# Gamma multiplied into B instead of C, a shorter chain of parameters and a new order in a fused S5 and H3 kernel

## The chip, the cores and the metric

The kernel runs on one core of a Trainium2 chip. Its engines are TensorE (PE, matmuls into the accumulators PSUM), VectorE (DVE), ScalarE (ACT), GpSimd (POOL) and SyncE (SP, which here only issues DMAs); ACT can issue DMAs as well. The metric is the device time of one execution in microseconds (us), the median of three runs.

## The reference

Two layers are computed on 2048 rows of 640 columns, and their results are put side by side (bf16, 2048 x 1280).

```python
Lam_bar = exp(dt * Lam)                              # A: a diagonal state-space layer (S5), 640 complex states
B_bar = ((Lam_bar - 1.0) / Lam)[:, None] * Bmat
Bu = einsum("bld,pd->blp", x, B_bar)
h[t] = Lam_bar * h[t - 1] + Bu[t]                    # 2048 steps
y_A = 2.0 * einsum("blp,dp->bld", h, Cmat).real + x * Dskip

kv = shift_conv(k, shift_k) * v                      # B: H3, four taps, then a long convolution of length 2048
y = irfft(rfft(kv, 4096) * rfft(ssm_k, 4096))[:2048] + kv * ssm_D
y_B = q * y
out = concatenate([y_A, y_B], axis=-1)
```

The factor of a state, 2(Lam_bar - 1)/Lam with the 2 of the output taken in, is called gamma below. Since the recurrence is diagonal, gamma can be multiplied into B or into C.

## The kernel before, in words

All data lie in one SBUF tile, `arena`, cut into named parts (A, BT, RR, Y, T, ...), and all accumulators in one PSUM tile, `acc`, of eight banks. `build` makes a list of some 800 operations; each names the engines that may run it and the pieces of `arena` that it reads and writes. `Program.depend` (L92) finds from the pieces which operation has to follow which. The string `ORDER` gives the order: every entry is the number of an operation, the engine (T for TensorE, V for VectorE, A for ScalarE, G for GpSimd, S for SyncE) and the first PSUM bank. `Program.emit` (L122) writes the program of each engine in this order, with a wait wherever a predecessor is on another engine. Every engine and every DMA queue runs what it has strictly in that order. Line numbers in the profile are of the operation's code; helpers that copy or scale (L198, L199) stand for many operations.

Part A, in the order of its data:

- The parameters (`params`, L338 on): TensorE turns Lambda and log_dt into columns (L356), VectorE copies them (L358), and a chain of small operations on 128 x 10 numbers makes the phases, the powers `al` of Lam_bar, gamma (`cf`), and from these the matrices that TensorE uses: `RR` (L436) for powers of Lam_bar, `GM` for gamma.
- `load_B` (L482): each of five blocks of B is loaded and turned by TensorE with an identity (L496, two groups of five transposes a block), evicted by L498 into `BT`. `warm` (L511) is eight matmuls ahead of it.
- The up-sweep: `up2` (L552, the base matmuls x·B, evicted by L568), `up1` (ten base matmuls and two of L571, evicted by L590) and `up0` (L552, L571, L612) build sums over 16 rows. The coarse scan (`coarse`, L619) swaps halves on TensorE (L639, L640), multiplies by cosines and sines on VectorE (L642 to L653) and scans (L647). The down-sweep (`down`, L672, L673; added by L690 or L692) fills in all states.
- `scale_C` (L531): ten groups of eight matmuls (L543) multiply gamma, as `GM`, into the loaded C; L547 evicts them into `CT`.
- `project` (L696): for each of 16 row sets ten matmuls for each half with C (L711), VectorE adds x·D (L715, with L701), and a DMA stores the rows (L719). Row set 13 comes last and is cut in two halves.

Part B makes kv (taps L198, sums L794 and L795), writes it to DRAM and reads it back in another layout, and does the long convolution by two matmul stages (`s1` L830 or L835, `s2` L854, evicted by L840 and L867), a product (L878 to L885) and two stages back (`r2` L899, `r1` L920, evicted by L904 and L932); L944 stores it. The same stages transform ssm_k. A group of `s1` has a wide form (16 matmuls over 128 rows, L830) and a narrow one (32 over 64 rows, L835); a lower-case t in `ORDER` asks for the narrow one. GpSimd makes the tables of phases (L289, L291, L327, L330) and takes some of the products.

The operations around `up2` are mixed with part B's kv on VectorE and ScalarE; `s1` and `s2` of ssm_k run between the up-sweep's and down-sweep's groups; part B's remaining stages run between the 16 projections.

## Time and profile before

| what | value |
|---|---|
| median of three runs | 193.33 us (193.14 to 193.49) |
| span of the profiled execution | 195.7 us |
| VectorE, ScalarE, GpSimd, share of the span | 84%, 72%, 40% |
| DMA, mean rate | 30.15 MB, 154 GB/s |
| base matmuls of the up-sweep (L552) | 220 in 47.8 us |
| projection (L711) | 320 in 45.7 us |
| gamma into C: TensorE (L543), VectorE's share of evictions (L547) | 80 in 4.3 us, 5 in 3.9 us |

The page of the profile gives busy time by engine and groups of instructions by line: the engine, the operation, its output and input, shapes (partitions x elements), count, busy time, mean ns of one, and the idle time of the engine in front of them with what released it. Timelines have the start, the duration, and the same names. In the windows a stretch of time has its length, and busy time and instructions of each engine.

### The profile page before, as it was taken

What the parts mean: (1) busy time and instruction counts of PE and PEld (TensorE: products, weight loads), DVE (VectorE), ACT (ScalarE), POOL (GpSimd) and SP (SyncE); (2) the same over time, 40 slices, a digit from 0 to 9 for tenths busy, and PEclk for the clock granted to TensorE, in tenths of its full rate; (3) what the DMA queues carried; (4) which work ended last, traced back from release to release, by engine and by line L of the source; (5) the groups of instructions that cost most, each with busy time, mean ns of one, the idle gap of its engine ahead of it and who ended that gap; (6) DMA issues with size and microseconds to landing.
All of it is one profiled execution on the core that took longest, in us unless ns stands there. A gap on an engine that the chain in (4) does not pass through costs nothing.

```text
span 195.7 us, 7455 instructions
## 1 busy us (share of the span) xinstructions
PE 181.7 (93%) x3297; PEld 120.1 (61%) x3300; DVE 165.3 (84%) x228; ACT 140.9 (72%) x170; POOL 78.1 (40%) x62
## 2 busy tenths in 40 slices
PE   7699699999999999889998999999999999999980
PEld 2586334444455666565676675557678776977750
DVE  4686999337999898999999999999999999969840
ACT  2499936999999899999988999888747750750000
POOL 8979940530030000196805480876050209302020
PEclk9999979999999999999999999999999999999998
DMA  5999869989699999979993899511199970536985
GB/s 153 259 195 176 135 131 151 185 131 135 129 249 183 243 244 123 156 149 152 126 138 147 208 189 158 106 36 35 35 219 184 189 155 3 134 107 157 211 192 154
DMA packets 103786, 30.15 MB, mean 154 GB/s; under 512 B 97482, under 2 KB 103114, under 8 KB 103754
## 3 DMA queue, kind: packets, MB, share of 16 engines
q1 hardware_dynamic: 103004, 28.86, 81.1%
q10 hardware_dynamic: 750, 0.82, 1.4%
q8 instruction: 26, 0.43, 0.9%
q14 instruction: 6, 0.05, 0.1%
HBM read 12.30 MB, written 7.86 MB: 103 GB/s over the span
## 4 chain that ended last, share of the span: by engine, by line
PE 69%; ACT 10%; DMA 8%; DVE 5%; issue 4%; SPq 2%; ACTq 0%; DVEq 0%
PE acc L711 21%; PE acc L552 19%; PE acc L899 6%; PE acc L854 5%; DMA arena<-in_B_ssm_k_dram 4%; PE acc L571 4%; ACT arena L867 4%; PE acc L835 4%; PE acc L673 3%; PE acc L920 3%; DMA arena<-in_A_B_re_dram 2%; SPq L761 2%; PE acc L830 2%; ACT arena L498 2%; PE acc L672 1%
## 5 line engine op out<-in xcount | busy, mean ns | idle before, releaser
L552 PE MATMUL acc<-arena 128*128 128x512 bf16 (+1 forms) x220 | 47.8, 375 | 1.9 <-DVE arena L402 1.9
L711 PE MATMUL acc<-arena 128*128 128x320 bf16 x320 | 45.7, 299 | 0.0
L867 ACT CAST arena<-acc 128x960 bf16<-128x960 f32 (+1 forms) x40 | 35.2, 907 | 7.0 <-PE acc L854 6.4
L711 PEld LDWEIGHTS <-arena 128*128 128x128 bf16 x320 | 30.4, 98 | 12.6 <-ACT arena L867 0.4
L552 PEld LDWEIGHTS <-arena 128*128 128x128 bf16 x220 | 21.9, 102 | 23.7 <-DVE arena L402 2.2
L840 ACT CAST arena<-acc 128x1024 bf16<-128x1024 f32 x32 | 31.1, 1027 | 2.0 <-PE acc L835 1.5
L904 ACT CAST arena<-acc 128x1024 bf16<-128x1024 f32 x16 | 15.6, 1029 | 10.8 <-PE acc L899 10.8
L854 PE MATMUL acc<-arena 128*64 128x160 bf16 x512 | 22.2, 235 | 0.4 <-ACT arena L867 0.3
L701 POOL TENSOR_TENSOR arena<-arena 128x640 bf16<-128x640 bf16 x8 | 11.7, 1473 | 26.1 <-DMA arena<-in_A_x_dram 26.1
L854 PEld LDWEIGHTS <-arena 128*64 128x64 bf16 x512 | 17.9, 109 | 5.8 <-issue 1.7
L794 POOL TENSOR_TENSOR arena<-arena 128x2048 bf16<-128x2048 bf16 x2 | 8.5, 4246 | 28.3 <-DVE arena L198 28.3
L715 DVE TENSOR_TENSOR arena<-acc,arena 128x640 bf16<-128x640 f32 (+1 forms) x17 | 13.1, 782 | 6.3 <-PE acc L711 6.1
L883 POOL TENSOR_TENSOR arena<-arena 128x1280 bf16<-128x1280 bf16 x4 | 11.3, 2824 | 16.7 <-DVE arena L881 11.0
L794 DVE TENSOR_TENSOR arena<-arena 128x2048 bf16<-128x2048 bf16 x13 | 16.0, 1233 | 1.3 <-ACT arena L199 1.2
L840 DVE CAST arena<-acc 128x1024 bf16<-128x1024 f32 x8 | 9.7, 1221 | 6.8 <-PE acc L835 6.7
L673 PE MATMUL acc<-arena 128*128 128x512 bf16 (+2 forms) x50 | 12.8, 327 | 0.0
L835 PEld LDWEIGHTS <-arena 64*64 64x64 bf16 x960 | 9.3, 107 | 4.9 <-issue 1.3
L881 POOL TENSOR_TENSOR arena<-arena 128x1280 bf16<-128x1280 bf16 x3 | 7.8, 2617 | 11.0 <-ACT arena L867 6.1
L932 DVE TENSOR_TENSOR arena<-acc,arena 128x960 bf16<-128x960 f32 (+1 forms) x12 | 11.9, 1036 | 0.0
L878 DVE TENSOR_TENSOR arena<-arena 128x2560 bf16<-128x2560 bf16 x8 | 11.9, 1483 | 0.0
L835 PE MATMUL acc<-arena 64*64 64x64 bf16 x960 | 11.3, 194 | 0.4 <-ACT arena L840 0.2
L692 DVE TENSOR_TENSOR arena<-acc,arena 128x1024 bf16<-128x1024 f32 (+1 forms) x10 | 11.1, 1137 | 0.5 <-PE acc L673 0.5
(143 smaller groups left out, 309.9 us busy)
## 6 DMA issues: line engine op xcount, KB each, us to landing
out_dram<-arena SPq DMA_DIRECT2D x31, 160.0 KB, 3.2
arena<-in_B_ssm_k_dram SPq DMA_DIRECT2D x8, 320.0 KB, 4.8
kv_rows<-arena SPq DMA_DIRECT2D x5, 512.0 KB, 3.9
arena<-kv_rows SPq DMA_DIRECT2D x16, 160.0 KB, 4.4
arena<-in_A_x_dram SPq DMA_DIRECT2D x16, 160.0 KB, 3.4
arena<-in_B_q_dram SPq DMA_DIRECT2D x8, 320.0 KB, 5.5
arena<-in_A_B_re_dram ACTq DMA_DIRECT2D x3, 160.0 KB, 3.4
arena<-in_A_B_im_dram SPq DMA_DIRECT2D x3, 160.0 KB, 3.5
```

The source lines that it names most:

```text
L552: e.matmul(o, lhsT=self.BT[j][:, d, :], rhs=self.XP[:, d, lo:lo + n], start=(d == 0), stop=(d == 4), skip_group_check=True)
L673: e.matmul(B[:, o], lhsT=c.RR[:, n, j, :], rhs=fr(j, q, k), start=not by_pe, stop=True, skip_group_check=True)
L711: e.matmul(B[:, 512 * (b - b0):512 * (b - b0) + 320], lhsT=lh[j], rhs=self.CT[:, j, 320 * b:320 * b + 320], start=(j == 0), stop=(j == 9))
L715: P.add(f"ev_C{i}", {PDVE: dve(320 * (b1 - b0))}, lambda e, B, part=part, n=b1 - b0: e.tensor_tensor(out=part.rearrange("p (b n) -> p b n" ...
L794: P.add(f"ca{d}_{j}", tt, lambda e: e.tensor_tensor(out=t1, in0=t1, in1=t2, op=ALU.add), outs=[t1], ins=[t1, t2])
L835: e.matmul(B[64 * b:64 * b + 64, 512 * l + 64 * i:512 * l + 64 * i + 64], lhsT=lh[i][ps], rhs=F[ps, b, 64 * l:64 * l + 64], start=True, st ...
L840: P.add(f"e1{what}{hf}_{u}", {PACT: act(1024), PDVE: dve(1024)}, lambda e, B: c.CP[e](out=out, in_=(B.rearrange("p (l n s k) -> p k s l n" ...
L854: e.matmul(B[64 * s:64 * s + 64, 512 * b + 160 * i:512 * b + 160 * i + 160], lhsT=c.W[:, k, 64 * b:64 * b + 64], rhs=self.AS[hf][:, k, 160 ...
L867: c.CP[e](out=out, in_=b.rearrange("p r (k j n) -> p r k j n", k=n, j=4) if nj > 1 else b.rearrange("p r (k x) -> p r k x", k=n))
L878: P.add(f"pp{hf}", n1, lambda e: e.tensor_tensor(out=pt, in0=X, in1=Yk, op=ALU.mult), outs=[pt], ins=[X, Yk])
L904: P.add(f"er2{hf}_{u}", {PACT: act(1024), PDVE: dve(1024)}, lambda e, B: c.CP[e](out=out, in_=B.rearrange("p (s n b) -> p b s n", s=2, n=4 ...
L932: e.tensor_tensor(out=Q, in0=B.rearrange("p (g x) -> p g x", g=2)[:, :, 0:80 * n].rearrange("p g (x n) -> p g x n", n=40), in1=Q, op=ALU.mult)
```

## The change

Gamma moves from C to B. A block of B is no longer turned with an identity; each half of its rows is multiplied by a 64 x 128 matrix made of gamma, so that turning and scaling are one step. It is 20 matmuls over 64 rows a block (two groups, of 16 and 4) with results in f32, where there were ten transposes. The evictions are of 1024 and 256 elements where there were two of 640. `scale_C` with its 80 matmuls and ten evictions goes. In its place `place_C` copies C into the states' layout: eight copies over 64 rows, five on VectorE (four of 2560 elements, one of 640) and three on ScalarE (640 each).

The chain of parameters gives 15 columns where it gave 10 (five more for the layout of B's rows), joins steps by two-scalar operations and `scalar_tensor_tensor`, makes powers by squaring (`rq`) instead of five exponentials, and makes the sine that gamma needs on ScalarE ahead of the phases' tables. `gm` is five small spreads, one a block, instead of one big one. The sign of the phase offsets turns, so the coarse scan adds where it subtracted, and the other way round.

Stores of the output (`st_A`, `st_B`) may be issued by ScalarE. In the new order 11 of 33 are. `ORDER` is new throughout; GpSimd loses three operations (two taps' sums and the spread of the scan's factor r16), VectorE gets them. Of 40 groups of `s1`, 17 are wide where 10 were; five of these seven come after the first projection. The last group of the up-sweep's L552 and two of five groups of `s2` that stood ahead of the coarse scan's first swap stand behind it now on TensorE.

```diff
-    ("PV", 60), ("SMALL", 1400)):
+    ("PV", 90), ("SMALL", 1500)):
...
+    sg = f(10).rearrange("p (x k) -> p x k", x=2)
+    for x, sc in ((0, PI), (1, TWO_PI)):
+        P.add("sg", {A: .2}, lambda e, x=x, sc=sc: e.activation(out=sg[:, x], in_=fr[:, 10:15], func=FN.Sin, scale=float(sc * EPS1)),
+              outs=[sg[:, x]], ins=[fr[:, 10:15]])
...
+    def gm(k):
+        P.add(f"gm{k}", {V: .42}, lambda e: e.tensor_tensor(
+            out=c.GM[:, k], in0=bc(c.E.rearrange("p (o m) -> p o m", o=1), [128, 4, 64]),
+            in1=bc(c4[:, :, k:k + 1], [128, 4, 64]), op=ALU.mult), outs=[c.GM[:, k]], ins=[c.E, c4[:, :, k:k + 1]])
+    for k in range(5):
+        gm(k)
...
-        for r in range(2):
-            g, part = P.group(1), raw[:, 640 * r:640 * r + 640]
...
-                for d in range(5):
-                    e.transpose(out=B.bitcast(bf16)[:, 128 * d:128 * d + 128], in_=part[:, 128 * d:128 * d + 128], identity=idn)
+        for d0, n in ((0, 4), (4, 1)):
+            g = P.group(2)
...
+                for d in range(d0, d0 + n):
+                    for r in range(2):
+                        for j in range(2):
+                            ps = slice(64 * j, 64 * j + 64)
+                            o = 512 * j + 128 * (d - d0)
+                            e.matmul(B[:, o:o + 128], lhsT=raw[ps, 640 * r + 128 * d:640 * r + 128 * d + 128],
+                                     rhs=c.GM[ps, k, 2 * r:2 * r + 2, :].rearrange("p x m -> p (x m)"), start=(r == 0), stop=(r == 1),
+                                     skip_group_check=True, tile_position=(64 * j, 0))
...
-    def scale_C(self, a, h):
...
+    def place_C(self):
+
+        c, P = self.c, self.c.P
+        T4 = self.CT.rearrange("p (a e) d -> p a e d", e=2)
+        for part, a0, n in ((0, 0, 4), (1, 4, 1)):
+            for e_ in range(2):
+                for r in range(2):
+                    to, fro = slice(64 * r, 64 * r + 64), slice(64 * e_, 64 * e_ + 64)
+                    out, src = T4[to, a0:a0 + n, e_], self.CRa[part][fro, r]
+                    P.add(f"mvC{part}{e_}{r}", {PDVE: .16 + .00026 * 640 * n, PACT: act(640 * n)}, lambda e, out=out, src=src: c.CP[e](out=out, in_=src),
+                          outs=[out], ins=[src])
...
-            P.add(f"st_A{i}", {PSP: .5}, lambda e, dst=dst, part=part: e.dma_start(out=dst, in_=part), ins=[part], nbytes=128 * 640 * (b1 - b0))
+            P.add(f"st_A{i}", {PSP: .5, PACT: .5}, lambda e, dst=dst, part=part: e.dma_start(out=dst, in_=part), ins=[part], nbytes=128 * 640 * (b1 - b0))
...
-    "162A0 98G0 48G0 73V0 0V0 11G0 75S0 5G0 4T0 12V0 13V0 76A0 6G0 14V0 163S0 17V0 36G0 168A0 74S0 31V0 1T1 32V0 24G0 15V0 55V0 "
+    "24G0 48G0 11G0 5G0 6G0 19V0 152S0 139V0 73V0 75S0 39G0 12V0 13V0 17V0 32V0 30V0 147S0 31V0 7V0 74A0 55V0 20G0 33V0 76A0 51V0 "
```

The first place is VectorE during the up-sweep's first pass. Before, its evictions are L568; L232, L256, L412 and L274 are small operations on tables and parameters, L498 evicts B.

```order
L232 TENSOR_TENSOR arena<-arena 128x64
L256 TENSOR_TENSOR arena<-arena 128x4
L412 TENSOR_SCALAR arena<-arena 128x10
L568 CAST arena<-acc 128x2x2x256
L402 MEMSET arena 64x1
L274 TENSOR_TENSOR arena<-arena 128x256
L498 COPY arena<-acc 128x10x64
L568 CAST arena<-acc 128x2x2x256
```

In the new kernel the same evictions are L588; L814 is a sum of taps of kv, L449 makes `al`, L456 spreads it into `RR`, and L272, L306, L256 and L274 are tables.

```order
L272 TENSOR_SCALAR arena<-arena 128x64
L306 TENSOR_SCALAR arena<-arena 128x192
L814 TENSOR_TENSOR arena<-arena 128x2048
L256 TENSOR_TENSOR arena<-arena 128x4
L274 TENSOR_TENSOR arena<-arena 128x256
L449 TENSOR_TENSOR arena<-arena 128x80
L588 CAST arena<-acc 128x2x2x256 x2
L456 TENSOR_TENSOR arena<-arena 128x1280
L588 CAST arena<-acc 128x2x2x256 x2
```

The evictions of this pass stand in one block behind the tables and `al`; before, small operations and evictions took turns, and B's own evictions stood among them.

The second place is VectorE between the coarse scan and the first projection's sum (L715 before, L735 after). Before: L547 evicts gamma·C, L642 and L653 belong to the scan, L692 to the down-sweep, L840 and L867 to ssm_k's transform, L198 to the taps.

```order
L547 CAST arena<-acc 128x2x320
L642 TENSOR_TENSOR arena<-acc,arena 128x640
L653 TENSOR_TENSOR arena<-arena 128x5x128
L692 TENSOR_TENSOR arena<-acc,arena 128x4x256
L547 CAST arena<-acc 128x2x320 x2
L840 CAST arena<-acc 128x64x2x8
L198 TENSOR_SCALAR arena<-arena 128x2048 x2
L701 TENSOR_TENSOR arena<-arena 128x640
L692 TENSOR_TENSOR arena<-acc,arena 128x256
L547 CAST arena<-acc 128x2x320 x2
L867 CAST arena<-acc 128x2x3x160 x2
L198 TENSOR_SCALAR arena<-arena 128x2048
```

After: L567 copies C, L673 is the scan's last step, L712 the down-sweep, L860 and L887 ssm_k's transform, L815 a sum of taps, L898 and L901 the product.

```order
L673 TENSOR_TENSOR arena<-arena 128x5x128
L815 TENSOR_TENSOR arena<-arena 128x2048
L712 TENSOR_TENSOR arena<-acc,arena 128x4x256
L198 TENSOR_SCALAR arena<-arena 128x2048 x2
L567 COPY arena<-arena 64x4x640
L860 CAST arena<-acc 128x64x2x8
L712 TENSOR_TENSOR arena<-acc,arena 128x256
L887 CAST arena<-acc 128x2x3x160
L887 CAST arena<-acc 128x2x2x160
L567 COPY arena<-arena 64x4x640 x3
L898 TENSOR_TENSOR arena<-arena 128x2560
L901 TENSOR_TENSOR arena<-arena 128x8x160
```

Five evictions out of PSUM gave way to four copies within SBUF, and a sum of taps that GpSimd made has come to VectorE.

The third place is the end of the two queues that store. Before, SyncE's last rows (L944 stores part B, L719 part A):

```order
L719 DMA out_dram<-arena 128x640
L944 DMA out_dram<-arena 32x16x160 x4
L719 DMA out_dram<-arena 128x640
L944 DMA out_dram<-arena 32x16x160 x2
L719 DMA out_dram<-arena 128x640
L719 DMA out_dram<-arena 128x320 x2
```

After, the end of ScalarE's program, where L924 is an eviction and L964 and L739 are the stores:

```order
L924 CAST arena<-acc 128x256x4 x6
L964 DMA out_dram<-arena 32x16x160
L924 CAST arena<-acc 128x256x4
L964 DMA out_dram<-arena 32x16x160 x4
L739 DMA out_dram<-arena 128x320 x2
```

Both halves of the last row set are now issued by ScalarE, which has nothing behind them; SyncE ends with six stores of part B and two whole row sets of part A.

152 lines of the change are left out of this document (71 added, 81 removed), and 74 rows, old and new, of the table ORDER.

## The prediction

> **What bounds the kernel now.** I read the page first, then the windows by stage, then the single engines' timelines at the three places where the new order changes most. The page:
>
> ```profile
> span 195.7 us, 7455 instructions
> PE 181.7 (93%) x3297; PEld 120.1 (61%) x3300; DVE 165.3 (84%) x228; ACT 140.9 (72%) x170; POOL 78.1 (40%) x62
> ```
>
> TensorE is busy for 93% of the span, so time goes only if its idle time, its half-clock time or its work goes. The span of this execution, 195.7, stands 2.4 us over the median of 193.33; I work out differences against the span and apply them to the median. About 0.2% (0.39 us, so 192.94 to 193.72) is what a measurement of this kernel tells from no change. By stage, each column busy time with its instructions:
>
> ```profile
> core 0: us, PE busy (x) PEld busy (x) DVE busy (x) ACT busy (x) POOL busy (x), PEclk, DMA share, GB/s
> 36.20:50.00 13.80, 13.80 (x187) 6.50 (x184) 6.58 (x11) 13.20 (x14) 4.51 (x3) 1.00 0.92 138
> 50.00:70.93 20.93, 20.77 (x345) 12.71 (x345) 19.59 (x26) 19.58 (x28) 1.54 (x1) 1.00 1.07 227
> 70.93:98.91 27.98, 26.07 (x585) 17.18 (x585) 26.48 (x33) 27.14 (x35) 13.20 (x3) 1.00 1.13 145
> 98.91:130.00 31.09, 29.79 (x715) 19.64 (x712) 29.67 (x32) 28.40 (x31) 16.65 (x8) 1.00 0.73 147
> 130.00:189.95 59.95, 59.91 (x1305) 46.12 (x1304) 53.61 (x62) 28.26 (x31) 17.21 (x9) 1.00 0.58 130
> ```
>
> From 36 to 71 and from 130 on TensorE has no gap: there only its work counts. Between 70.93 (the coarse scan's first swap is on TensorE) and 98.91 (the first projection, C0) it idles 1.9 us while VectorE is busy for 26.48 of 27.98 and ScalarE for 27.14: this stretch is set by the two that evict. Ahead of 36 lies the other loss, TensorE's timeline of the start:
>
> ```profile
> 7.71 4.45 PE L496 MATMUL acc<-arena 128*128 128x128 bf16 x40 [1.79 <-DMA arena<-in_A_B_re_dram]
> 11.96 9.68 PE L552 MATMUL acc<-arena 128*128 128x256 bf16 x60
> 23.58 14.81 PE L552 MATMUL acc<-arena 128*128 128x512 bf16 x60 [1.95 <-DVE arena L402]
> 38.23 0.59 PE L571 MATMUL acc<-arena 128*128 128x512 bf16 x2
> ```
>
> The up-sweep's first pass (L552) starts at 11.96 when all of B is turned, stands for 1.95 us before 23.58, and its second pass (first L571, behind ten base matmuls) comes at 38.23.
>
> **The start.** The new kernel cannot turn B before gamma is known. The price of one step of the parameters' chain:
>
> ```profile
> 4.89 0.19 DVE L358 COPY arena<-acc 128x30 f32<-128x30 f32 x1 [1.46 <-PE acc L356]
> ...
> 12.45 0.17 DVE L375 TENSOR_SCALAR arena<-arena 128x10 f32<-128x10 f32 x1
> ```
>
> By the new program some 27 VectorE instructions stand between the parameters' copy and the first blocks of gamma, at 0.17 each (L375), from 4.9, the first turn can start at about 9.5. A turn of one block is now 20 matmuls over 64 rows, two at a time; the nearest row, 24 matmuls of 160 columns that also use half of the array, is the 1.02 us at 69.49 (quoted below): 0.0425 each, 0.034 at 128 columns, so 0.7 us a block and up to 1.4 at half clock. With its eviction of 1.2 (as L568 below), a second one for the block's last fifth (0.4) and some 0.7 of waits between these steps the first L552 comes at about 13.2, **1.2 us later** than 11.96. Three more blocks, 2.1 us, are turned between matmuls of L552. What goes is the gap and what follows it:
>
> ```profile
> 23.90:27.30 3.40, 3.40 (x10) 1.22 (x9) 3.37 (x5) 0.28 (x1) 3.01 (x2) 0.50 0.19 39
> 27.30:30.70 3.40, 3.40 (x18) 1.50 (x16) 3.31 (x4) 3.01 (x3) 0.00 (x0) 1.00 1.36 215
> ```
>
> Behind the gap the granted clock is 0.50 for 3.4 us: 10 matmuls instead of 18, eight of 0.19 us (3.40/18), 1.5, and I take 1.7 with the edges of the stretch. Nor is the pass's beginning at full rate:
>
> ```profile
> L552 PE MATMUL acc<-arena 128*128 128x256 bf16 x40 | 5.7, 301 | 0.0
> ```
>
> Forty of its first 60 matmuls have 256 columns, 20 have 512. At 0.219 for 512 (ten from 66.77 to 68.96, below) and half of it for 256 they need 8.8 and took 9.68: 0.9. From 11.96 to 38.23 are 26.3 us; less the gap (2.0), the half clock (1.7) and this 0.9, 21.7 are left. So without any gap the second pass's first L571 comes at 13.2 + 21.7 + 2.1 = 37.0, with 0.2 for small waits **1.0 earlier** than 38.23.
>
> Is there a gap? That of before came so:
>
> ```profile
> 20.45 1.92 POOL L291 TENSOR_TENSOR arena<-arena 128x1024 int32<-128x1024 int32 x1
> ...
> 20.53 1.86 DVE L412 TENSOR_SCALAR arena<-arena 128x10 f32<-128x10 f32 x1
> 22.31 1.21 DVE L568 CAST arena<-acc 128x1024 bf16<-128x1024 f32 x1
> ```
>
> A ten-element VectorE operation stood as long as GpSimd's multiply of tables, and the eviction that frees a bank of accumulators stood behind it. The new order has the same constellation later: a convolution's product (L814 of the new kernel), a table product (L274) and the coefficients `al` (L449) are ahead of two evictions of L552 on VectorE, while GpSimd makes tables. The bounds are no wait, and two multiplies in a row (3.8). I take one wait of 1.9, less 0.3 that TensorE still has ahead: +1.6, too short, I choose, to drop the clock. **Front: −1.0 + 1.6 = +0.6** (bounds −3.8, if the later start hides, to +4.5, two multiplies and one half-clock stretch: −1.0 + 3.8 + 1.7).
>
> Two rules of the Trainium skill bear on this. SBUF — State Buffer, § Who interferes with whom: a VectorE instruction with two SBUF inputs stands for the whole of a GpSimd instruction that reads SBUF, one with at most one such input and no two-port mode does not. It speaks against this change, as `al` and the convolution's product have two such inputs; by it the front is +0.6 or worse. L412 has one tensor input and stood as well, in a two-port mode by that page. TensorE: Matmul & The Clock Gate, § Part 1: The HAM clock gate: an idle window of about 3.4 us halves the clock, windows run freely. The trace agrees with the length (3.40 at 0.50), but a pause of 2.0 sufficed here; by the rule a gap of 1.6 costs no clock (total 190.8), by the trace's case it may cost the half stretch too (192.8).
>
> **Up to C0.** TensorE's rows before the swap:
>
> ```profile
> 66.77 2.36 PE L552 MATMUL acc<-arena 128*128 128x512 bf16 x10
> 68.96 0.60 PE L571 MATMUL acc<-arena 128*128 128x256 bf16 x4
> 69.49 1.02 PE L854 MATMUL acc<-arena 128*64 128x160 bf16 x24
> 70.67 0.22 PE L640 MATMUL acc<-arena 128*128 128x128 bf16 x1 [0.16 <-issue]
> ```
>
> The up-sweep's last base group (66.77 to 69.49, 2.7) and two of five L854 groups (0.9) now stand behind the swap: TensorE is there 3.5 earlier. VectorE had 6.58 + 19.59 = 26.2 us of work in the 34.7 from 36.2 to 70.93; the order brings some 3.5 forward, 29.7, which at the 94% of the window from 50 on end at 36.2 + 31.6 = 67.8. TensorE is ready at 67.2; I take 67.5 for the swap's product on VectorE instead of 70.9. From there to C0 VectorE sets the pace. Its groups in this stretch:
>
> ```profile
> L547 DVE CAST arena<-acc 128x640 bf16<-128x640 f32 x5 | 3.9, 814 | 0.0
> L840 DVE CAST arena<-acc 128x1024 bf16<-128x1024 f32 x3 | 3.6, 1221 | 0.4 <-PE acc L835 0.4
> ...
> L198 DVE TENSOR_SCALAR arena<-arena 128x2048 bf16<-128x2048 bf16 x4 | 2.9, 744 | 0.0
> ...
> L878 DVE TENSOR_TENSOR arena<-arena 128x2560 bf16<-128x2560 bf16 x1 | 1.5, 1483 | 0.0
> L794 DVE TENSOR_TENSOR arena<-arena 128x2048 bf16<-128x2048 bf16 x1 | 1.2, 1215 | 0.0
> ```
>
> Out go the five evictions of gamma·C (3.9), one L840 (1.2), one L198 (0.75), one L878 (1.5) and small ones (0.9): 8.3. In come an L198 (0.75), three tensor products as L794 (3.6), small ones (1.5) and four copies of C over 64 rows, 2560 elements each. Such a copy the trace does not show: as L198 it takes 744·2560/2048 = 0.93, as L794 1.5, at the rate of evictions (L840) 3.0. The nearest is L198, one input and both ends in SBUF: 3.7 together. In: 9.5. So 28.0 becomes 29.2 and C0 comes at 67.5 + 29.2 = 96.7: **−2.2**. The 80 matmuls of gamma·C on TensorE, 4 us, give nothing here, since VectorE ends last; if it no longer does, they are what is gained on top. ScalarE loses five evictions and gets three short copies, so it does not take over.
>
> **After C0.** Five more of part B's first transforms stand in the wide form:
>
> ```profile
> 130.12 0.64 PE L830 MATMUL acc<-arena 128*64 128x128 bf16 x16
> 130.69 0.71 PE L835 MATMUL acc<-arena 64*64 64x64 bf16 x64
> 131.33 2.89 PE L711 MATMUL acc<-arena 128*128 128x320 bf16 x20
> ```
>
> Wide takes 0.57, narrow 0.64 for two: 0.25 more each, +1.3. Between 98.91 and 130 TensorE idled 1.3 and VectorE loses about 1.5 of work: I take half, −0.7. **Net +0.6** (bounds 0 to +1.3).
>
> **The end.** VectorE's last sum and SyncE's stores, then the short stores from issue to landing:
>
> ```profile
> 189.97 0.49 DVE L715 TENSOR_TENSOR arena<-acc,arena 128x320 bf16<-128x320 f32 x1 [0.76 <-PE acc L711]
> 190.88 1.91 SPq L719 DMA_DIRECT2D out_dram<-arena  x3
> ...
> out_dram<-arena SPq DMA_DIRECT2D x2, 80.0 KB, 2.9
> ```
>
> Three stores queue on SyncE, 1.91 us from 190.88; the last, a third of them, starts at about 192.2, lands 2.9 later, and the span ends 0.6 after that: 195.7, 5.75 after TensorE's end at 189.95. Now the last half block's store is ScalarE's, which is idle at the end, and starts 0.15 after the sum: 0.49 + 0.15 + 2.9 + 0.65 = 4.2 after TensorE. **−1.55** (bounds −1.2, if SyncE's two remaining stores end last, to −2.0).
>
> Sum: 0.6 − 2.2 + 0.6 − 1.55 = −2.55, on 193.33 **190.8**.
>
> **The rivals.**
> No wait at the start: front −1.0, sum −4.15, 189.2; 186.4 if the later start hides as well. For it: evictions from PSUM are not held themselves, and ScalarE shares them. Against it: three VectorE operations of the held kind stand ahead of the evictions.
> One wait with the half clock: front +2.6, 192.8. For it: 2.0 us did it before. Against: windows may fall otherwise.
> Slower: the evictions wait for two multiplies of GpSimd in a row (3.8) and TensorE's clock halves once more, front +4.5, 194.7. It decides once the front costs over 3.5 us, since the other terms give −3.15. For it: GpSimd's tables stand in the new order between the same operations, and L412 waited for a whole multiply. Against it: GpSimd has 14 us less work and before it happened once.
> C's copies at the rate of L794 or of evictions: +2.3 to +8.3 before C0, 193.1 to 199. For it: they cross from one half of the partitions to the other. Against it: L198's type and rate.
> Nothing but the end gains, since VectorE's lead-in isn't fed at 94%: 193.33 − 1.55 = 191.8.
>
> **How the numbers follow.** My forecast 0.40 (its own range 189.9 to 191.9); no wait 0.24; half clock 0.12; two multiplies 0.13; slow copies 0.07; the end alone 0.04. The range leaves out the extreme of no wait (below 187.8) and half of the two slow cases (above 194.5). Faster: 0.40 + 0.24 + 0.07 of the half clock + 0.01 of the copies + 0.04 = 0.76. Within 0.2%: 0.04 + 0.03 + 0.01 = 0.08. Slower: 0.12 + 0.03 + 0.01 = 0.16.
>
> **What would show it.** The start: the first L552-type matmul at about 13, the first of the second pass at 38.8, and the granted clock of 15 to 40; a half-clock stretch there tells the rivals apart. Up to C0: the swap's product at 67.5 to 68 and C0 at about 97 when front is taken off; the copies of C at 0.93 each. After C0: seventeen wide transforms and TensorE without gaps. The end: the span 4.2 us behind the last matmul, its last store on ScalarE. Wrong if C0 stands at 99 or later, or if the end stays at 5.7.

## The result and the profile after

The changed kernel is slower: 199.84 us (median of 6 runs, 198.50 to 200.45) against 193.24 us (6 runs, 192.94 to 193.51), a ratio of 1.032 with a 95% interval of 1.029 to 1.036. That is outside the predicted range.

Its page, first lines:

```profile
span 196.6 us, 7185 instructions
PE 178.5 (91%) x3157; PEld 118.5 (60%) x3160; DVE 165.4 (84%) x236; ACT 138.8 (71%) x159; POOL 71.8 (37%) x58
```

The profile of before that the prediction was made from turned out to be of an unusual execution. A span stands 1.8 to 1.9 us below its execution's time here (see the pairs that follow), so 195.7 belongs to a time of about 197.5, where the median is 193.24. The unchanged kernel was therefore profiled once more (experiment 0): span 190.8. Both this profile and the one of after are of the fastest execution of their set (192.64 us of ten, 198.50 of six), so these two are compared from here on; their spans differ by 5.8, where the medians differ by 6.6.

Four landmarks on TensorE cut both spans: the first base matmul of the second pass (L571 before, L591 after, as every line of the new kernel is some 20 higher), the end of the last one, the projection's first matmul (C0; L711, L731), and TensorE's end. First the windows of the unchanged kernel between them, then those of the changed one; each column is busy time with its instructions.

```profile
core 0: us, PE busy (x) PEld busy (x) DVE busy (x) ACT busy (x) POOL busy (x), PEclk, DMA share, GB/s
0.00:34.34 34.34, 29.55 (x180) 15.43 (x180) 29.09 (x66) 27.10 (x37) 27.24 (x40) 1.00 1.08 185
34.34:73.85 39.51, 39.24 (x592) 22.20 (x593) 32.17 (x45) 36.68 (x45) 5.97 (x4) 1.00 1.09 186
73.85:95.02 21.17, 19.37 (x514) 13.32 (x516) 20.52 (x26) 20.53 (x27) 13.19 (x3) 1.00 1.06 149
95.02:185.62 90.60, 89.75 (x2018) 65.79 (x2016) 82.91 (x93) 56.50 (x62) 33.85 (x16) 1.00 0.65 139
```

```profile
0.00:39.77 39.77, 31.16 (x231) 17.08 (x232) 25.99 (x76) 25.52 (x32) 29.29 (x41) 1.00 0.98 181
39.77:79.27 39.50, 39.09 (x587) 22.38 (x589) 35.60 (x44) 36.25 (x44) 5.20 (x2) 1.00 0.91 183
79.27:99.59 20.32, 16.35 (x407) 12.12 (x408) 19.12 (x24) 19.38 (x23) 6.23 (x2) 1.00 1.01 159
99.59:193.60 94.01, 91.91 (x1936) 66.89 (x1936) 84.23 (x94) 57.67 (x63) 31.11 (x14) 1.00 0.59 128
```

Length less TensorE's busy time is its idle time:

| stretch | before | after | difference | of it TensorE busy | idle |
|---|---|---|---|---|---|
| front, to the second pass | 34.34 | 39.77 | +5.43 | +1.61 | +3.82 |
| second pass | 39.51 | 39.50 | −0.01 | −0.15 | +0.14 |
| its end to C0 | 21.17 | 20.32 | −0.85 | −3.02 | +2.17 |
| C0 to TensorE's end | 90.60 | 94.01 | +3.41 | +2.16 | +1.25 |
| behind TensorE's end | 5.2 | 3.0 | −2.2 | | |
| span | 190.8 | 196.6 | +5.8 | +0.6 | +7.4 |

TensorE's busy time is nearly the same in all (177.9, 178.5): C's turns are gone, but the front and the stretch behind C0 take more. B's turns are not the reason: the front of run 3 below, with the same turns, has TensorE busy for 29.2 us, and what the changed kernel has on top of that, about 1.9, is work at half speed, as the next rows show. Idle time is the larger part of the loss, half of it in the front. TensorE's timeline there, before (experiment 0) and after; the bracket is the wait ahead of a group and what ended it:

```profile
10.71 1.25 PE L552 MATMUL acc<-arena 128*128 128x256 bf16 x10 [0.16 <-ACT arena L498]
12.33 16.56 PE L552 MATMUL acc<-arena 128*128 128x512 bf16 x90 [0.37 <-DMA arena<-in_A_x_dram]
30.01 4.49 PE L552 MATMUL acc<-arena 128*128 128x512 bf16 x20 [1.12 <-DVE arena L568]
```

```profile
4.33 3.60 PE L538 MATMUL acc<-arena 128*128 128x512 bf16 x8 [0.31 <-DVE arena L258]
12.28 3.17 PE L520 MATMUL acc<-arena 64*128 64x128 bf16 x56 [4.36 <-DVE arena L416]
15.38 2.93 PE L572 MATMUL acc<-arena 128*128 128x512 bf16 x10
...
26.77 13.16 PE L572 MATMUL acc<-arena 128*128 128x512 bf16 x80 [0.23 <-DVE arena L524]
39.77 0.59 PE L591 MATMUL acc<-arena 128*128 128x512 bf16 x2
```

TensorE waits 4.36 us for gamma (L416), and the first base matmul comes 4.7 us later than before (15.38, 10.71). No gap follows at the place where the prediction had one, but the first matmuls are slow: 56 of B's turns take 3.17 us where the same 56 take 1.88 in run 3, and the first ten base matmuls 2.93 where they take 2.32 there. The clock column can't show this here, because this profile has no record of the clock ahead of 16.63 us and the column counts such time as 1.00. In run 4, which has the record from 8.53 on, the same 56 turns, behind a wait of 4.01, stand in a stretch at half clock (0.50):

```profile
11.94:15.35 3.41, 2.94 (x56) 2.90 (x56) 3.41 (x8) 1.01 (x1) 2.36 (x3) 0.50 1.16 205
```

So the front's +1.61 of busy time is the half clock. Why gamma is late stands in ScalarE's timeline of the changed kernel:

```profile
8.47 0.33 ACTq L507 DMA_DIRECT2D arena<-in_A_B_im_dram  x1
8.85 0.22 ACT L374 ACTIVATE arena<-arena 128x15 f32<-128x15 f32 x1 [4.33 <-DMA arena<-in_A_B_re_dram]
```

L374 is the exponential of gamma's chain. It needs no B, but in ScalarE's queue it stands behind the issue of a load of B. In the trace the DMA issues of SyncE and ScalarE take eight semaphores in turn, and the one that this issue takes was last taken by another load of B, which SyncE issues only behind a transposing load of x:

```profile
3.03 2.11 SPq L546 DMA_TRANSPOSE arena<-in_A_x_dram  x1
5.18 0.57 SPq L507 DMA_DIRECT2D arena<-in_A_B_re_dram  x1
```

So ScalarE stands until that load has landed, the releaser that the bracket of L374 names.

The other lines that answer to those shown of before: C's copies (L567), with mean ns, and the kernel's end.

```profile
L567 DVE COPY arena<-arena 64x2560 bf16<-64x2560 bf16 x4 | 3.3, 822 | 0.1
```

```profile
193.64 0.49 DVE L735 TENSOR_TENSOR arena<-acc,arena 128x320 bf16<-128x320 f32 x1 [0.53 <-PE acc L731]
```

```profile
190.70 3.82 ACTq L739 DMA_DIRECT2D out_dram<-arena  x2
```

### The profile page after: what moved, and what is told of

Read it like the earlier page. It is cut to its first block, busy times and chain, and to the rows that moved or that the text cites. A ratio compares the mean times of both kernels' runs of the same rounds, so it can differ in the third digit from the quotient of the medians.

```text
span 196.6 us, 7185 instructions
## 1 busy us (share of the span) xinstructions
PE 178.5 (91%) x3157; PEld 118.5 (60%) x3160; DVE 165.4 (84%) x236; ACT 138.8 (71%) x159; POOL 71.8 (37%) x58
## 4 chain that ended last, share of the span: by engine, by line
PE 63%; DVE 15%; ACT 10%; DMA 5%; issue 4%; SPq 1%; ACTq 0%; DVEq 0%
PE acc L572 21%; PE acc L731 16%; PE acc L591 4%; ACT arena L860 4%; PE acc L874 4%; PE acc L693 3%; ACT arena L887 3%; PE acc L919 3%; PE acc L850 3%; PE acc L855 3%; DMA arena<-in_A_B_re_dram 3%; PE acc L940 2%; DVE arena L735 2%; PE acc L520 2%; DVE arena L901 2%
## 5 line engine op out<-in xcount | busy, mean ns | idle before, releaser
L572 PE MATMUL acc<-arena 128*128 128x512 bf16 (+1 forms) x220 | 46.2, 363 | 0.3 <-DVE arena L524 0.2
L731 PE MATMUL acc<-arena 128*128 128x320 bf16 x320 | 45.7, 299 | 0.5 <-DVE arena L567 0.4
L731 PEld LDWEIGHTS <-arena 128*128 128x128 bf16 x320 | 30.4, 98 | 13.3 <-ACT arena L887 1.0
L860 ACT CAST arena<-acc 128x1024 bf16<-128x1024 f32 x35 | 34.0, 1025 | 3.9 <-PE acc L855 3.4
L887 ACT CAST arena<-acc 128x960 bf16<-128x960 f32 (+1 forms) x38 | 34.0, 924 | 3.2 <-PE acc L874 2.4
L721 POOL TENSOR_TENSOR arena<-arena 128x640 bf16<-128x640 bf16 x6 | 8.5, 1430 | 58.5 <-DMA arena<-in_B_ssm_D_dram 36.9
L924 ACT CAST arena<-acc 128x1024 bf16<-128x1024 f32 x17 | 16.7, 1024 | 12.2 <-PE acc L919 12.0
L901 POOL TENSOR_TENSOR arena<-arena 128x1280 bf16<-128x1280 bf16 x4 | 10.9, 2730 | 21.1 <-DVE arena L898 21.0
L735 DVE TENSOR_TENSOR arena<-acc,arena 128x640 bf16<-128x640 f32 (+1 forms) x17 | 13.2, 783 | 6.3 <-POOL arena L721 2.9
L814 DVE TENSOR_TENSOR arena<-arena 128x2048 bf16<-128x2048 bf16 x14 | 17.1, 1219 | 0.8 <-ACT arena L199 0.5
L198 DVE TENSOR_SCALAR arena<-arena 128x2048 bf16<-128x2048 bf16 x16 | 13.3, 841 | 0.2
L898 DVE TENSOR_TENSOR arena<-arena 128x2560 bf16<-128x2560 bf16 x8 | 11.9, 1485 | 0.3
L905 POOL TENSOR_TENSOR arena<-arena 128x1280 bf16<-128x1280 bf16 x2 | 6.3, 3165 | 15.7 <-ACT arena L924 13.2
L710 ACT CAST arena<-acc 128x1024 bf16<-128x1024 f32 (+2 forms) x11 | 10.0, 948 | 2.5 <-PE acc L693 2.3
L919 PE MATMUL acc<-arena 64*128 64x128 bf16 x320 | 11.7, 225 | 0.0
L291 POOL TENSOR_TENSOR arena<-arena 128x1024 int32<-128x1024 int32 x4 | 8.8, 2208 | 7.4 <-DVE arena L285 7.4
L712 DVE TENSOR_TENSOR arena<-acc,arena 128x1024 bf16<-128x1024 f32 (+1 forms) x10 | 11.1, 1139 | 0.4 <-PE acc L693 0.4
```

Of the source, the lines that this page charges most:

```text
L198: vm = lambda e: lambda out, in_, by: e.tensor_scalar_mul(out=out, in0=in_, scalar1=by)
L572: e.matmul(o, lhsT=self.BT[j][:, d, :], rhs=self.XP[:, d, lo:lo + n], start=(d == 0), stop=(d == 4), skip_group_check=True)
L731: e.matmul(B[:, 512 * (b - b0):512 * (b - b0) + 320], lhsT=lh[j], rhs=self.CT[:, j, 320 * b:320 * b + 320], start=(j == 0), stop=(j == 9))
L735: P.add(f"ev_C{i}", {PDVE: dve(320 * (b1 - b0))}, lambda e, B, part=part, n=b1 - b0: e.tensor_tensor(out=part.rearrange("p (b n) -> p b n" ...
L814: P.add(f"ca{d}_{j}", tt, lambda e: e.tensor_tensor(out=t1, in0=t1, in1=t2, op=ALU.add), outs=[t1], ins=[t1, t2])
L860: P.add(f"e1{what}{hf}_{u}", {PACT: act(1024), PDVE: dve(1024)}, lambda e, B: c.CP[e](out=out, in_=(B.rearrange("p (l n s k) -> p k s l n" ...
```

## The experiments

Landmarks of all profiled executions, from TensorE's timelines, in us; "pass", "chain" and "rest" are the three differences between the first four:

| kernel | 1st L591 | last L591 | C0 | PE end | span | pass | chain | rest | median | ratio |
|---|---|---|---|---|---|---|---|---|---|---|
| before again (0) | 34.34 | 73.85 | 95.02 | 185.62 | 190.8 | 39.51 | 21.17 | 90.60 | 194.05 | 1.000 ± 0.003 |
| after | 39.77 | 79.27 | 99.59 | 193.59 | 196.6 | 39.50 | 20.32 | 94.00 | 199.84 | 1.032 ± 0.004 |
| 1 load behind sines | 41.04 | 80.46 | 100.79 | 194.62 | 198.1 | 39.42 | 20.33 | 93.83 | 201.43 | 1.041 ± 0.004 |
| 2 before, end on ScalarE | 34.41 | 73.92 | 95.14 | 186.94 | 193.8 | 39.51 | 21.22 | 91.80 | 196.64 | 1.013 ± 0.005 |
| 3 all of B first | 37.34 | 80.16 | 100.48 | 195.78 | 199.0 | 42.82 | 20.32 | 95.30 | 199.58 | 1.032 ± 0.005 |
| 4 narrow as before | 39.90 | 80.20 | 100.52 | 200.28 | 203.3 | 40.30 | 20.32 | 99.76 | 204.50 | 1.056 ± 0.004 |
| 5 stores on SyncE | 39.98 | 79.49 | 99.82 | 194.27 | 198.8 | 39.51 | 20.33 | 94.45 | 201.16 | 1.040 ± 0.005 |
| 6 B turned at once | 41.50 | 80.92 | 101.24 | 195.06 | 198.2 | 39.42 | 20.32 | 93.82 | 201.19 | 1.039 ± 0.005 |
| 7 three back to GpSimd | 39.76 | 81.22 | 104.97 | 199.81 | 203.4 | 41.46 | 23.75 | 94.84 | 205.75 | 1.062 ± 0.004 |
| 8 taps ahead of turns | 39.38 | 79.52 | 99.84 | 194.03 | 197.4 | 40.14 | 20.32 | 94.19 | 200.03 | 1.036 ± 0.005 |
| 9 product on VectorE | 40.05 | 79.53 | 102.77 | 196.94 | 200.2 | 39.48 | 23.24 | 94.17 | 202.37 | 1.046 ± 0.003 |
| 10 tables early | 37.42 | 78.25 | 98.56 | 193.88 | 197.1 | 40.83 | 20.31 | 95.32 | 199.32 | 1.030 ± 0.007 |
| 11 product late | 40.22 | 79.63 | 99.57 | 195.39 | 199.0 | 39.41 | 19.94 | 95.82 | 200.54 | 1.034 ± 0.010 |
| 12 less VectorE work | 39.94 | 79.36 | 99.44 | 193.67 | 197.1 | 39.42 | 20.08 | 94.23 | 199.28 | 1.032 ± 0.007 |
| 13 less ScalarE work | 40.09 | 79.51 | 99.84 | 194.43 | 197.6 | 39.42 | 20.33 | 94.59 | 200.24 | 1.029 ± 0.011 |
| 14 less of both | 40.26 | 79.69 | 99.10 | 193.87 | 197.5 | 39.43 | 19.41 | 94.77 | 199.40 | 1.024 ± 0.006 |
| 15 less behind C0 | 39.84 | 79.32 | 99.64 | 193.73 | 196.9 | 39.48 | 20.32 | 94.09 | 199.48 | 1.029 ± 0.008 |

Ratios are to the unchanged kernel on the same chip, with half of their 95% interval. The times of one kernel scatter by a us or more; what is read below is the stages. "Chain" repeats to 0.1 us in the versions whose edits lie elsewhere, and so does "pass" in most of them. "Rest" does not: it is 93.8 to 95.8 in versions whose edits lie ahead of C0, and 90.6 to 91.8 in the profiles of the old kernel. So the loss behind C0 is clear, its size is known to about 1 us, and differences of a us in "rest" are not read.

In the diffs that follow, a token of ORDER is an operation's number, its engine (T, V, A, G, S; t for TensorE is a transform in the narrow form) and its accumulator bank.

**0. The unchanged kernel again**, no edit.

> The kernel before, unchanged, for a second profile. Every run of the changed kernel has its span 1.8 to 1.9 us below its time, but the profile of before has a span of 195.7 beside a median of 193.2, so an ordinary execution of before should span about 191.4. Theory A: the 4.3 us between are the gap of TensorE at 21.5 with the half clock behind it, and an ordinary execution has neither; then the first L571 stands at about 34.5 and the first projection at about 95. Theory B: the start is as in the first profile (first L571 at 38) and the 4.3 us lie later.

The windows above are its. The second pass begins at 34.34, not 38.23; TensorE's gap ahead of its last base group is 1.12 us, and the granted clock is 1.00 in every stage. The profile that the prediction used was 3.9 us later at this landmark, of 4.9 in all; 0.4 of the others lie behind C0 and 0.6 behind TensorE's end. Of the 3.9, 1.25 lie ahead of the first base matmul (11.96, 10.71), 0.5 are a longer wait within the pass (1.95, against 0.37 and 1.12), and the other 2.2 are matmuls that ran slower.

**1. The load moved behind the sines**: what does the DMA issue on ScalarE cost?

```diff
-129G0 165A0
+88A0 165A0
```

> The changed kernel with one DMA issue moved on ScalarE's queue: the load of B's fourth block (imaginary half) from ahead of the exponential r1 to behind the two sines. Theory A (the issue waited for an earlier transfer, 4.3 us, and r1 and all of gamma stood behind it): the first turn moves from 12.3 to about 9.5, the time falls by 2 to 3 us, to 197 to 198. Theory B (the later start of the turns is taken up anyway in the stretch from 70 to 100, where VectorE sets the pace): the first turn moves but the time falls by less than 1 us.

Gamma is early as the theory says (the first turn at 8.34), but it brings nothing, for the next wait is right behind it, on TensorE:

```profile
8.34 1.43 PE L520 MATMUL acc<-arena 64*128 64x128 bf16 x40 [0.28 <-DVE arena L416]
15.61 1.04 PE L520 MATMUL acc<-arena 64*128 64x128 bf16 x16 [5.84 <-DMA arena<-in_A_B_im_dram]
```

B's last parts now come too late, the clock is 0.50 from 11.93 to 18.76, and the pass begins at 41.04. The time rises, to 201.43: both theories missed, as neither had B's landing in it.

**3. All of B ahead of x on SyncE**, to take both waits away.

```diff
+75S0 147S0 146S0 164S0 165S0 140S0 141S0 152S0 153S0
```

> The changed kernel with all loads of B ahead of all loads of x: eight of the ten on SyncE directly behind Lambda's load, in the order in which the blocks are turned, none on ScalarE behind the first two. Theory A (the start is set by B's loads that wait behind x's transposing loads and, on ScalarE, hold up the parameters' chain): the first turn at about 8.5, no wait for B behind it, the first base matmul at 11.5 to 12.5 instead of 15.4, the second pass's first L591 at 36 to 37 instead of 39.8, and the time falls by about 3 us, to 196 to 197.5. Theory B (x comes later by as much, or the stretch up to the first projection takes it up): L591 at 39 or the first projection unmoved at 99.6, within 1 us of 199.8.

The first turn starts at 8.58, no half clock is in the record, which begins at 8.11, and the pass begins 2.4 us earlier, at 37.34. TensorE still waits there, 3.4 us, now for x, whose loads stand behind B's:

```profile
8.58 1.88 PE L520 MATMUL acc<-arena 64*128 64x128 bf16 x56 [0.31 <-DVE arena L416]
12.35 2.32 PE L572 MATMUL acc<-arena 128*128 128x512 bf16 x10 [1.89 <-DMA arena<-in_A_x_dram]
14.60 0.73 PE L520 MATMUL acc<-arena 64*128 64x128 bf16 x20
16.87 4.49 PE L572 MATMUL acc<-arena 128*128 128x512 bf16 x20 [1.54 <-DMA arena<-in_A_x_dram]
```

The second pass then takes 42.82 instead of 39.50: k's second load is issued at 36.11, behind v's, which waits for tables whose temporaries lie in v's buffer, and ScalarE waits for it:

```profile
41.87 2.00 ACT L199 ACTIVATE arena<-arena 128x2048 bf16<-128x2048 bf16 x1 [2.30 <-DMA arena<-in_B_k_dram]
```

**6 and 8** varied this front: all of B turned before the first base matmul (besides 3's loads, B's turns and their evictions in one block), and 3 with ScalarE's first tap and two evictions ahead of others (`+9A0 365A0`, `145V2` and `157V0` to ScalarE).

> As the run with all of B's loads first, and in addition all five blocks are turned ahead of the first base matmul, so that VectorE's evictions of the last two blocks no longer stand in its queue for turns that TensorE makes between base matmuls. Theory A (up to the second product of part B the time is set by VectorE, and what the start costs is VectorE's idle time, not TensorE's late start: it waited 7.4 us for turns in the run with the loads first, 5.8 in the changed kernel): VectorE's waits for turns fall below 2 us, the first taps start at about 18 instead of 22, the first projection stands at 95 to 97, and the time falls by 3 to 5 us, to 195 to 197. Theory B (the end of the up-sweep on TensorE sets the first projection): L591 at about 37 as in that run, the first projection at 99.5 to 100.5 and the time within 1 us of 199.6.

> As the run with all of B's loads first, but the evictions of the last two blocks' small turns are ScalarE's instead of VectorE's, and ScalarE's first tap of kv stands ahead of its evictions there. Theory A (up to the second product VectorE's queue sets the time; what the start costs is VectorE's time behind late turns, 7.4 us in that run): VectorE's first tap starts at about 18.5 instead of 22, its waits for turns fall below 2 us, v's first load starts 2 or more earlier than 31, the first projection stands at 96 to 98.5, and the time falls by 2 to 4 us against that run, to 195.5 to 197.5. Theory B (something else than the start sets the first projection, such as the loads of k and v in SyncE's queue): the first tap moves but the first projection stays at 99.5 to 100.5.

In 6, which missed its aim, TensorE waits 3.7 us for VectorE's evictions of B (L524) and 1.1 for ScalarE's, the clock is 0.50 from 13.61 to 20.43, and the pass begins at 41.50. Eight loses what it wins: VectorE waits 4.5 us for a table of ScalarE's (L273) and 3.3 for k, and C0 stands at 99.84.

**10. As 3, and the small tables and v's load early.**

```diff
+103V0 25V0 27V0 52V0 21V0
+138A0 28A0 53A0
+29V0 145V2
+173S0 363S0
```

> All of B first, as before, and besides the small integer tables (L269, L272, L306, L256, L273, L274), whose temporaries lie where v is loaded, made in VectorE's idle time near 13 to 18 us, and v's first load issued behind x's, so that k's second load comes some 5 us earlier. Theory A (the 2.4 us that the earlier first turn won were lost because the loads of v and k wait behind these tables, and the engines then wait for k): the wait of ScalarE's tap for k (2.3 us in that run) goes, VectorE loses less than 1 us to k instead of 4.2, and the projection's first matmul of the sum comes at 97.5 to 98.5 instead of 100.5; the time is 197 to 198. Theory B (that stretch is filled by VectorE's own work, and whatever wait goes is taken by the next one): that matmul stays at 99.5 to 100.5, the time at 199 to 201.

The best of the fronts: C0 at 98.56, 1.0 us earlier than after and 1.9 than 3, at the edge of A's range; the time stayed with B's, and "rest" is 1.3 longer than after's, which is within its scatter. TensorE waits 2.9 us for x in its front. Its timelines also show what the tables cost on VectorE while GpSimd multiplies. VectorE's and GpSimd's rows here, and VectorE's of the same table in 3:

```profile
14.24 1.84 DVE L272 TENSOR_SCALAR arena<-arena 128x64 int32<-128x64 int32 x1
16.00 2.00 DVE L306 TENSOR_SCALAR arena<-arena 128x192 int32<-128x192 int32 x1
```

```profile
14.14 3.74 POOL L291 TENSOR_TENSOR arena<-arena 128x1024 int32<-128x1024 int32 x2
```

```profile
27.28 0.25 DVE L306 TENSOR_SCALAR arena<-arena 128x192 int32<-128x192 int32 x1
```

**7. Three operations back to GpSimd** (the spread of the scan's factor, a sum of taps, L814, and the product with v, L815, which stands above as a sum of taps).

```diff
-299V0 436V0 437V0
+299G0 436G0 437G0
```

> The changed kernel with the three operations that VectorE took over from GpSimd given back to it at the same places of the order: the spread of the scan's factor and two sums of taps, 3.9 us of VectorE's work. Theory A (VectorE sets the pace up to the second product): 1.5 to 3.5 us less, 196.5 to 198.3, the first projection 1.5 or more earlier. Theory B (a slow GpSimd sum of 4.2 us holds up VectorE's next tap or the scan by as much): within 1 us of 199.8.

C0 is 5.4 us later. A copy that takes 0.31 us elsewhere stood as long as GpSimd's sum:

```profile
76.12 4.18 DVE L567 COPY arena<-arena 64x640 bf16<-64x640 bf16 x1
...
87.89 3.17 DVE L670 TENSOR_TENSOR arena<-arena 128x640 bf16<-128x640 bf16 x1
```

```profile
75.89 4.23 POOL L814 TENSOR_TENSOR arena<-arena 128x2048 bf16<-128x2048 bf16 x1 [8.84 <-DVE arena L198]
...
85.47 5.24 POOL L815 TENSOR_TENSOR arena<-arena 128x2048 bf16<-128x2048 bf16 x1
```

VectorE's two operations end within 0.2 and 0.4 us of GpSimd's. TensorE waits 1.88 and 3.12 us for VectorE behind them, and each wait is followed by 3.4 us at a clock of 0.50.

**9 and 11. The first D·x on VectorE** instead of GpSimd (`697G0` to `697V0`), in its place and, in 11, behind the down-sweep's first part (`325V2 697V0`): is the second scan slow (2.57 us, the first 1.48) because GpSimd works beside it?

> The changed kernel with one product (x times D of the first row set, L721) on VectorE as before instead of GpSimd. It runs at 81.85 to 83.4 on GpSimd, where VectorE's second scan (L667) takes 2.57 us instead of 1.48. Theory A (the scan has two SBUF inputs and stood behind GpSimd's product): the second scan takes about 1.5, VectorE pays 0.5 for the product, the first projection comes 0.4 to 0.7 earlier and the time falls by 0.3 to 0.8 us. Theory B (the scan is long for its data or by a wait of its own): it stays at 2.5 and the time rises by 0 to 0.5.

> The first product D times x (L721) on VectorE instead of GpSimd, as in the run where VectorE waited 2.34 us for x at that place, but now put behind the down-sweep's first part, where x has long come. Theory A (while GpSimd makes it, VectorE's scan is held, 2.57 us instead of 1.48): the scan takes 1.5 again, the product 0.5 of VectorE's own, and the projection's first matmul of the sum comes 0.4 to 0.8 earlier than 99.6. Theory B (the scan is slow for another reason): the scan stays at 2.6 and that matmul comes at 100.1 or later.

It is: with GpSimd idle the second scan takes 1.49 in both, as in this row of 11.

```profile
82.57 1.49 DVE L667 TENSOR_TENSOR_SCAN arena<-arena 128x640 bf16<-128x640 f32 x1
```

In 9 VectorE waited 2.34 us for x at the product's place, so C0 came later. In 11 the chain is 0.38 shorter than after's, less than the 1.08 of the scan, because VectorE then waits for TensorE and makes the product itself.

**12, 13, 14. Less work ahead of C0**: VectorE's, ScalarE's, both.

```diff
-            P.add(f"ca{d}_{j}", tt, lambda e: e.tensor_tensor(out=t1, in0=t1, in1=t2, op=ALU.add), outs=[t1], ins=[t1, t2])
+            P.add(f"ca{d}_{j}", tt, lambda e: e.tensor_tensor(out=t1[:, :n], in0=t1[:, :n], in1=t2[:, :n], op=ALU.add), outs=[t1], ins=[t1, t2])
...
+        m = lambda e, x: x[:, :, :, :, 0:1] if what == "k" and hf == 0 and e is c.nc.scalar else x
```

(n is 64 for block 3; cx3 likewise; m is put round both operands of ScalarE's copies L860.)

> Leaves out most of block 3's sums of taps and its product with v: three L814 and one L815 on VectorE between the coarse scan and the projection's sum go over 64 columns instead of 2048 (1.2 us each now). Theory A (this stretch is bound by VectorE's work, of which the new order put 2.4 us more there, and that is why the 3.4 us won in the second pass do not arrive): the projection's first matmul of the sum comes 3 to 4 us earlier than 99.59, at 95.6 to 96.6, and the time is 196 to 197. Theory B (TensorE's own chain, or a load, sets that matmul): it comes less than 1 us earlier.

> Leaves out seven eighths of the columns of ScalarE's eight evictions L860 for ssm_k (about 1 us each now), which all stand between the last base matmul (L591) of the second pass and the projection's sum. In the runs so far that stretch took 20.1 to 20.3 us whatever came before it, and 0.2 to 0.4 less when VectorE had less to do. Theory A (ScalarE's evictions hold TensorE's transforms and, behind them in TensorE's queue, the scan's products): the stretch falls to 17 or 18 us. Theory B (the scan and down-sweep themselves, a chain of short steps between VectorE and TensorE, set it): it stays above 19.7 us.

> The three edits of this stretch together: the eight short evictions on ScalarE, block 3's sums and product on VectorE over 64 columns, and the product D times x (L721) late on VectorE, so that GpSimd does not hold the scan. Theory A (two engines full of evictions): the stretch falls to 15 or 16 us. Theory B (the chain of scan and down-sweep): it falls only by the scan's 1.1 us and what stands between its steps on VectorE, to 18 or 19 us.

My theory A failed three times. With four operations of VectorE shortened by about 1 us each, C0 moved by 0.15. Three of the four lie ahead of the last base matmul; there VectorE just waited for TensorE, which has the moved base group to do, at the scan's second half:

```profile
78.34 0.45 DVE L632 CAST arena<-acc 128x256 bf16<-128x256 f32 x1 [3.62 <-PE acc L591]
```

Only the product (L815, 1.03 us shorter) lies in the 20 us up to C0. Of it 0.24 reached C0, and 0.71 became a wait for the down-sweep's matmuls on TensorE:

```profile
88.83 1.23 DVE L712 TENSOR_TENSOR arena<-acc,arena 128x1024 bf16<-128x1024 f32 x1 [0.71 <-PE acc L693]
```

Shorter evictions on ScalarE left the chain at 20.33, so these are not what sets it. All three edits made it 19.41: VectorE has 1.6 us less to do there (1.03 by the product, 1.08 by a scan that GpSimd no longer holds, less 0.48 for making L721 itself), and 0.9 of it arrived. That fits a chain of short steps between VectorE and TensorE, the coarse scan's second half, its swaps and the down-sweep, with C's copies as its last step (C0 waits 0.41 for L567 in the changed kernel and in all three). But VectorE is busy for 19.12 of the 20.32 us in the changed kernel, and only some 2 us of its work were taken away, so it is not excluded that its own work sets part of them.

**15. Less VectorE work behind C0** (as 12, for block 4 and VectorE alone), and **4. the wide transforms undone there** (seven tokens such as `602T0` to `602t0`, two the other way, so five fewer are wide).

> Leaves out most of block 4's last two sums of taps and its product with v on VectorE (two L814 and one L815 over 64 columns instead of 2048), all between the projection's first row set and its second sum; 3 us of VectorE's work. In the changed kernel VectorE has no wait from 99.4 to 124.4 there. Theory A (behind the first sum VectorE's work sets the pace, and the new order put work there, which is the 3.4 us lost from the first sum to the end): the third row set's first matmul, 22.3 us behind the first one's now, comes 2 to 3 us earlier, and of it at least 1.5 us arrive at TensorE's end (94.0 us behind the first sum now). Theory B (no such bound): the third row set moves less than 0.7 us.

> The changed kernel with the first transforms behind the first projection (s1 of the second half) in the forms that they have before: five fewer wide ones. Theory A (behind the first projection TensorE's work sets the time, 0.25 us for each wide one): 1.0 to 1.5 us less, 198.3 to 198.8. Theory B (TensorE waits there for evictions and banks, and the wide form only fills waits): within 0.5 of 199.8.

Fifteen: VectorE waits 3.05 us at its next sum instead, and "rest" is 94.09. Four: windows from C0 to the projection's last full row group, of before again, after, and 4.

```profile
95.02:156.62 61.60, 60.78 (x1335) 43.42 (x1333) 58.85 (x66) 50.55 (x56) 24.69 (x11) 1.00 0.69 139
```

```profile
99.59:163.24 63.65, 62.14 (x1252) 44.17 (x1253) 61.27 (x68) 50.78 (x56) 24.14 (x10) 1.00 0.59 122
```

```profile
100.52:164.43 63.91, 61.49 (x1332) 43.54 (x1333) 61.44 (x68) 50.75 (x56) 23.52 (x10) 1.00 0.60 126
```

The narrow form takes 0.65 us off TensorE and gives it back as idle time, 2.42 instead of 1.51, most of it for ScalarE's evictions. The rest of 4's loss came late: TensorE paused for 3.47 us at 182.14 and ran at half clock from 186.02 to 189.43. Two late products of GpSimd waited 13.84 and 7.19 us for x, whose load stood on SyncE behind stores; that this made the pause is likely, not shown.

**5. All stores on SyncE** (11 tokens, A to S, so that all 33 are there), and **2. the unchanged kernel with its last store on ScalarE** (`785S0` to `785A0`): what is the end worth by itself?

> The changed kernel with all 33 stores of the output on SyncE, in the same order. Theory A (ScalarE's stores gain at the end and cost nothing elsewhere): the span ends 5.2 instead of 3.0 us behind TensorE, so about 2 us slower, 201.5 to 202. Theory B (stores that wait on ScalarE hold up evictions and, by the shared set of eight DMA semaphores, SyncE's transfers, which costs TensorE between the first projection and its end as much as the end gains): within 0.7 of 199.8, with TensorE's end 1 us or more earlier than 94.0 behind the first projection.

> The kernel before with only the last store (second half of the last row set of part A) issued by ScalarE instead of SyncE. Theory A (three stores in a row on SyncE set the end): the end comes 1.2 to 2.0 us earlier, 191.2 to 192.0. Theory B (the landing sets the end whoever issues): within 0.4 of 193.2.

From TensorE's end to the span's takes 4.5 us with all stores on SyncE, 3.0 in the changed kernel. The same idea in the old kernel is a loss of 1.3% (interval 0.8 to 1.7%). SyncE's queue of it, then of before again:

```profile
185.51 4.11 SPq L944 DMA_DIRECT2D out_dram<-arena  x2
189.72 0.96 SPq L719 DMA_DIRECT2D out_dram<-arena  x2
```

```profile
184.71 1.03 SPq L944 DMA_DIRECT2D out_dram<-arena  x2
185.84 1.96 SPq L719 DMA_DIRECT2D out_dram<-arena  x3
```

By the order of the issues SyncE's second store of that pair takes the semaphore that ScalarE's store has taken before it; ScalarE issues that only at 187.50, when the sum is made, and SyncE stands until it has landed, 4.11 us instead of 1.03. A further 1.2 us lie between C0 and TensorE's end ("rest"), no more than its scatter.

## Why the prediction was wrong

1. **The baseline.** "I work out differences against the span and apply them to the median" took the profile's extra 2.4 us as spread over the whole. They were more, 4.2 (a time of about 197.5 against 193.33), as a span is not a time; and 3.9 of the 4.9 by which this profile exceeds the second one lie in the front. The gap and the half clock behind it belong to them, and the next step credited their end to the change ("What goes is the gap and what follows it"). In the ordinary execution the second pass begins at 34.34, with a wait of 1.12 and no half clock, so 3.9 of the front's gain were never there to be had. This is the largest error.
2. **The start.** The first turn was put at 9.5 and the first base matmul at 13.2; they came at 12.28 and 15.38. The count of VectorE's steps was a us too long, if anything (8.34 once ScalarE's DMA issue is out of the way). What failed is that I read only the engine that computes gamma, not the queue of the engine that makes its exponential, nor when B and x land; and of a half clock behind the wait for gamma the sum has 0.7 (a block at 1.4 instead of 0.7), where it took 1.9. The pass began at 39.77, 1.0 later than the forecast 38.8. The wait of 1.9 behind GpSimd at L588 did not occur; the rival without a wait was right in that. VectorE was held by GpSimd elsewhere: two spreads of gamma (L416) took 1.78 and 1.41 us instead of 0.42 beside GpSimd's tables, the second scan 2.57 instead of 1.49. That the pass began only 1.0 late is luck: the first base matmul was 2.2 late, and the wait of 1.6 that was to follow it did not come.
3. **Up to C0.** The swap's product on VectorE (L662, at 69.08) came 29.3 us behind the second pass's beginning instead of 32.7, so the 3.4 forecast came true at this place. But 2.7 of them were the base group that had been moved behind the swap, and the scan's second half needs that group. Counted to its last base matmul, the pass takes 39.5 us in both. From the product to C0 were forecast 29.2 instead of 28.0; it took 30.5:

```profile
69.08:99.59 30.51, 26.29 (x511) 18.30 (x512) 28.73 (x37) 29.35 (x37) 6.23 (x2) 1.00 0.98 162
```

So the failing step is "From there to C0 VectorE sets the pace". VectorE's work grew by 2.2 us (28.73, 26.48), more than the 1.2 of the sum; half of that, 1.1, is the scan held by GpSimd, a term put at nothing. And the pace is not VectorE's alone: in run 12 the work taken from it came back as waits for TensorE. C0 came at 99.59, past the prediction's own mark of 99. The stretch gave 0.85 instead of 2.2, and the 80 matmuls of gamma·C, which had filled TensorE's waits in it, became idle time (+2.17). Of C's copies the size was right (0.82, forecast 0.93).
4. **After C0**: +0.6 forecast, +3.4 measured. TensorE's added work was right in sign (+1.3 forecast for the wide forms; they take 1.1 more, of +2.2 busy in all), but the idle time that I took off grew by 1.25. Up to 163.24 the loss is 2.05 (63.65 − 61.60): 1.36 of work and 0.69 of idle time, of which waits for ScalarE's evictions make some 0.4 (1.0 instead of 0.6). Neither wide forms (4) nor VectorE (15) nor the stores (5) explain it alone; which placement in the new order does stays open.
5. **The end**: −1.55 forecast, −2.2 measured. ScalarE's last store starts right behind the sum, as forecast. But with all stores on SyncE (5) the end, 4.5, is already 0.6 shorter than before, so the engine that issues makes 1.5 of it, and the rest comes with the new order; and in the old kernel the same move of the last store costs time (2).

The sum, −2.55, becomes +5.8: 3.9 by the baseline, 1.0 by the start, 1.3 by the chain, 2.8 behind C0, less 0.65 at the end. Two prices of rivals do not follow from the rows given: a front of −3.8 with a hidden later start (the later start is 1.2 in the same sum, so −2.2), and the half clock's 192.8, which has a wait of 1.9 where the forecast has 1.6. What the Trainium skill says in SBUF — State Buffer, § Who interferes with whom, is that VectorE in a two-port mode contends with GpSimd, that the one that issues first has the shared ports for its whole instruction, and that the other is blocked for so long. The trace agrees in 7, where a copy took 4.18 instead of 0.31 us; in the changed kernel the scan beside GpSimd's product took 1.1 us longer, of which 0.4 reached C0 (11).

Does the idea cost the time, or the order around it? No run here has gamma in B under the old order. With B first (3, 10) the front still costs 3.0 us more than before. In both TensorE waits there for x, 3.4 and 2.9 us, and not for gamma; no run had both B and x in time, so whether another order of the loads takes these 3 us away stays open. C's turns, which the change made superfluous, had mostly filled waits of TensorE: without their 80 matmuls the stretch up to C0 is 0.85 shorter. No version tried beats the kernel before; the nearest with all of its work is 10, at 1.030 ± 0.007, not to be told from after's 1.032.
